# Pinning TensorE to program order in a routed-attention and feed-forward kernel, with the second product in twos and the row maxima in the ffn's PSUM banks

## The chip, the cores and the metric

The kernel runs on one core of a Trainium2 chip. A core has five engines with a queue each: TensorE (PE in the profile; its weight loads are shown as PEld), VectorE (DVE), ScalarE (ACT), GpSimd (POOL) and SyncE (SP), which here only issues DMAs. The metric is the device time of one execution in microseconds (us), lower is better.

## The reference

Routing attention over B=4 batches, H=8 heads, S=768 positions, D=64, then a feed-forward block over the 3072 tokens with 512 features:

```python
q_assign = argmax(normalised q . normalised centroids)      # 16 clusters
k_assign = argmax(normalised k . normalised centroids)
mask = q_assign[:, :, :, None] == k_assign[:, :, None, :]
scores = where(mask, scale * q @ k.T, -1e9)
attn = exp(scores - scores.max(-1)); attn /= attn.sum(-1) + 1e-9
x = (attn @ v)  as (B*S, H*D)
h = x @ w_in                                   # 512 -> 2048
out = (h * erf(softplus(h))) @ w_out           # 2048 -> 512
```

## The kernel before

Heads are worked two at a time: a *pair* p of 16, four to a batch. A pair has 12 *units* u (two halves of 384 query columns, six key tiles j each), and the main loop takes two units per iteration, 96 iterations in all. In the kernel's text, and so in the order in which it emits instructions, one iteration is:

- `scores(u)`, `scores(u + 1)`: four matmuls each into a two-bank PSUM tile `sc` of pool `ps_s` (two buffers). Two are float32 (q times k), two bf16, which add the cluster mask and a shift. ACT then writes the exponential into `pr`, one of eight buffers, and POOL adds it into `acc`.
- `attend` of the six units before, when j is 0: twelve `av` products, the sums `psum` (from `acc`), the reciprocal `den` and the writing of `xT`, the attention output that is the ffn's input. `av` has one PSUM buffer; `psum` shares a single one (tag `t`) with all transposes.
- five *slots*. Each calls `pump`, which takes ffn matmuls from the generator `stream` to about 3340 cycles' worth (`owed` carries what is over or under); `prepare`, which advances the conversion of the weights (32 steps, on ACT, DVE and POOL); and one step of `aside(p + 1)`.

`aside(p + 1)` readies the next pair in 22 steps. `route` does four steps of transposing q and k (`pt`, with three ACT copies each), `psim` against the centroids, the transposes of `sims`, a chain over DVE and POOL to the one-hot masks `aq` and `ak`, and their transposes `pb` into `qm` and `km`. `shift` does twelve steps, each two bf16 products `sm` and one DVE maximum `nmx`; then `nm`, its transpose `pn`, and a DMA to DRAM (`line`) and two back into `qm`. The next pair's second score product needs that row.

The ffn works in 12 chunks of 256 tokens, three to a batch. `hidden(n)` is 64 products `hp` with w_in, then `gate(n)` on ACT and DVE; `project(n)` is 32 products `po` with w_out. Both take PSUM from `ps_f`, two banks. The stream yields nothing until all four pairs of the batch are done; from the 17th product of a chunk on, it mixes in two products of the chunk before's `project` for each `hp`. `xT` has few buffers: chunk c of pair p takes the slot of pair p - 5 (p - 6 for the third chunk), and waits until that one's `hidden` has read it.

The framework's scheduler sets the final order in each engine's queue when the program is built. The order of emission is a priority; an instruction that the scheduler takes to be ready may go ahead of earlier ones that it takes to be waiting. This holds for all engines.

The lines that the prediction names: L242 `pt`, L251 and L253 their copies, L260 `psim`, L270 the transposes of `sims`, L275 to L287 the chain on DVE (POOL in between), L301 `pb`, L311 the copy to `km`, L323 `sm`, L327 `nmx`, L332 `nm`, L337 `pn`, L364 and L370 the scores, L375 the exponential, L379 and L383 `acc`, L394 `av`, L401 `psum`, L405 and L406 `den`, L415 `xT`, L433 and L435 the gate, L454 `hp`, L475 `po`, and L155 the last step of a weight conversion.

Of the kernel before, what the change touches and what calls it, by code (L numbers as in the profile page):

```python
# [8 lines left out]
F32 = mybir.dt.float32  # L9
# [8 lines left out]
P = 128  # L18
# [25 lines left out]
def kernel(  # L44
# [8 lines left out]
    out: bass.AP,  # L53
):
    nc = tc.nc

    def pool(name, bufs, **kw):
        return ctx.enter_context(tc.tile_pool(name=name, bufs=bufs, **kw))
# [159 lines left out]
    for e in range(2):  # L218
        nc.vector.tensor_scalar_mul(out=cn[:, e], in0=cen, scalar1=rden)
    pct = ps_t.tile([P, P], F32, name="pct", tag="t")  # L220
    nc.tensor.transpose(out=pct, in_=cn.rearrange("p e d -> p (e d)"), identity=ident)
    for e in range(2):
        nc.vector.tensor_copy(
            out=ccT[e * D : (e + 1) * D, :, e * C : (e + 1) * C],
# [8 lines left out]
    def route(p):  # L233
        st = pairs[p]
        for nm in "qk":
            raw = rowp.tile([P, S], F32, name=nm + "T")

            low = rowp.tile([P, 2, S], BF16, name=nm + "m")
            for half in range(2):
                pt = ps_t.tile([P, HJ, P], F32, name="pt", tag="t")  # L240
                for jj in range(HJ):
                    nc.tensor.transpose(  # L242
                        out=pt[:, jj], in_=st[nm][:, HJ * half + jj].rearrange("p e d -> p (e d)"),
                        identity=ident,
                    )
                cols = slice(half * HW, (half + 1) * HW)
                src = pt.rearrange("p j t -> p (j t)")
                own = [(slice(e * D, (e + 1) * D), low[(1 - e) * D : (2 - e) * D, e, cols]) for e in range(2)]
                for r, dst in [(slice(0, P), raw[:, cols])] + own:
                    if nm == "q":  # L250
                        nc.scalar.mul(out=dst, in_=src[r], mul=D**-0.5)  # L251
                    else:
                        nc.scalar.copy(out=dst, in_=src[r])  # L253
                yield
            st[nm + "T"], st[nm + "m"] = raw, low
            del st[nm]
        load_qk(p + 1)
        psim = ps_t.tile([P, HW], F32, name="psim", tag="t")
        for g in range(4):
            nc.tensor.matmul(  # L260
                psim[2 * C * g : 2 * C * (g + 1)], lhsT=ccT[:, p % HP],
                rhs=st["qk"[g // 2] + "T"][:, (g % 2) * HW : (g % 2 + 1) * HW],
                start=True, stop=True,
            )
        sims = routep.tile([P, HW], F32, name="sims")
        nc.scalar.copy(out=sims, in_=psim)
        yield
        pt = ps_t.tile([P, HJ, P], F32, name="pt", tag="t")
        for jj in range(HJ):
            nc.tensor.transpose(out=pt[:, jj], in_=sims[:, jj * P : (jj + 1) * P], identity=ident)  # L270

        n = HJ * 8
        sim = pt.rearrange("p j (g c) -> p (j g) c", c=C)
        mx = routep.tile([P, n], F32, name="mx")
        nc.vector.reduce_max(out=mx, in_=sim, axis=AX.X)  # L275
        oh = sims.rearrange("p (g c) -> p g c", c=C)
        nc.vector.tensor_tensor(
            out=oh, in0=sim, in1=mx.unsqueeze(2).to_broadcast([P, n, C]), op=ALU.is_equal
        )

        nc.gpsimd.tensor_tensor(
            out=oh, in0=oh, in1=rank.unsqueeze(1).to_broadcast([P, n, C]), op=ALU.mult
        )
        mr = routep.tile([P, n], F32, name="mr")
        nc.vector.reduce_max(out=mr, in_=oh, axis=AX.X)
        for i, (dst, op) in enumerate(((aq, ALU.is_equal), (ak, ALU.not_equal))):
            nc.vector.tensor_tensor(  # L287
                out=dst.rearrange("p j h e c -> p j (h e) c")[:, :, :, 0:C],
                in0=oh.rearrange("p (j x g) c -> p j x g c", j=HJ, x=2)[:, :, i],
                in1=mr.rearrange("p (j x g) -> p j x g", j=HJ, x=2)[:, :, i].unsqueeze(3).to_broadcast(  # L290
                    [P, HJ, 4, C]
                ),
                op=op,
            )
        yield
        yield

        for nm, src in (("qm", aq), ("km", ak)):
            pb = ps_t.tile([P, NJ, P], BF16, name="pb", tag="t")
            for j in range(NJ):  # L300
                nc.tensor.transpose(  # L301
                    out=pb[:, j], in_=src[:, j % HJ, j // HJ].rearrange("p e c -> p (e c)"),
                    identity=identb,
                )
            for e in range(2):
                r = slice(e * D, (e + 1) * D)
                src = pb[r].rearrange("p j t -> p (j t)")
                if nm == "qm":
                    nc.vector.tensor_scalar_mul(out=st[nm][r, e], in0=src, scalar1=-BIG)
                else:  # L310
                    nc.scalar.copy(out=st[nm][r, e], in_=src)  # L311
            yield
# [3 lines left out]
    def shift(p):  # L316
        st = pairs[p]
        nmx = small.tile([P, NJ, 2, 2], F32, name="nmx")
        for t in range(NJ):
            for half in range(2):  # L320
                sm = ps_s.tile([P, 2, 512], F32, name="sm", tag="s")
                for e in range(2):
                    nc.tensor.matmul(  # L323
                        sm[:, e, 0:HW], lhsT=st["qm"][:, e, t * P : (t + 1) * P],
                        rhs=st["km"][:, e, half * HW : (half + 1) * HW], start=True, stop=True,
                    )
                nc.vector.tensor_reduce(  # L327
                    out=nmx[:, t, half], in_=sm[:, :, 0:HW], axis=AX.X, op=ALU.max, negate=True
                )
                yield  # L330
        nm = small.tile([P, 2, NJ], BF16, name="nm")
        nc.vector.scalar_tensor_tensor(  # L332
            out=nm.rearrange("p e t -> p t e"), in0=nmx[:, :, 0], scalar=FLOOR, in1=nmx[:, :, 1],
            op0=ALU.min, op1=ALU.min,
        )
        pn = ps_t.tile([2 * NJ, P], BF16, name="pn", tag="t")
        nc.tensor.transpose(out=pn, in_=nm.rearrange("p e t -> p (e t)"), identity=identb)  # L337
        nmT = small.tile([2 * NJ, P], BF16, name="nmT")
        nc.scalar.copy(out=nmT, in_=pn)
        line = linep.tile([2 * NJ, P], BF16, name="line")  # L340
        nc.sync.dma_start(out=line, in_=nmT)
        for e in range(2):
            r = e * D + SH
            nc.sync.dma_start(
                out=st["qm"][r : r + 1, e],
                in_=line[e * NJ : (e + 1) * NJ].rearrange("(o t) p -> o (t p)", o=1),
            )
        load(p, "v", v, vp)
        yield
# [7 lines left out]
    def scores(u):  # L357
# [3 lines left out]
        cols = slice(half * HW, (half + 1) * HW)  # L361
        for e in range(2):
            r = slice(e * D, (e + 1) * D)
            nc.tensor.matmul(  # L364
                sc[:, e, 0:HW], lhsT=st["kT"][r, j * P : (j + 1) * P], rhs=st["qT"][r, cols],
                start=True, stop=False,
            )
        for e in range(2):
            r = slice(e * D, (e + 1) * D)
            nc.tensor.matmul(  # L370
                sc[:, e, 0:HW], lhsT=st["km"][r, e, j * P : (j + 1) * P], rhs=st["qm"][r, e, cols],
                start=False, stop=True,
            )
# [10 lines left out]
                out=st["acc", half], in0=st["acc", half], in1=pr[:, :, 0:HW], op=ALU.add  # L384
            )

    def attend(u0):

        p, half, _ = units[u0]
        st = pairs[p]  # L390
        av = ps_v.tile([P, HW + 2], F32, name="av")
        for j in range(NJ):
            for e in range(2):
                nc.tensor.matmul(  # L394
                    av[e * D : (e + 1) * D], lhsT=st["v"][:, j, e], rhs=prs[(u0 + j) % NPT][:, e],
                    start=(j == 0), stop=(j == NJ - 1),
                )

        psum = ps_t.tile([P, HW], F32, name="psum", tag="t")
        for e in range(2):  # L400
            nc.tensor.matmul(  # L401
                psum[e * D : (e + 1) * D], lhsT=ones, rhs=st["acc", half][:, e], start=True, stop=True
            )
        den = routep.tile([P, HW], F32, name="den")
# [4 lines left out]
        while lo < (half + 1) * HW:  # L409
            c = lo // TB  # L410
            hi = min((c + 1) * TB, (half + 1) * HW)
            if c not in x:
                x[c] = xTp.tile([P, TB], F32, name=f"xT{c}", bufs=XBUFS[c])
            own = slice(lo - half * HW, hi - half * HW)
            nc.vector.scalar_tensor_tensor(  # L415
# [4 lines left out]
        if half == 1:  # L420
            xTs[p] = pairs.pop(p)["x"]


    TJ = TB // P
    CPB = S // TB

# [17 lines left out]
    def hidden(n):  # L444
        b, c = n // CPB, n % CPB
        gs[n] = gp.tile([P, NFT, TB], F32, name="g")
        for fp in range(NFT // GW):
# [3 lines left out]
            for a in range(GW):  # L451
                f0 = (fp * GW + a) * P
                for r in range(HP):
                    nc.tensor.matmul(  # L454
                        hp[:, a], lhsT=w_in[:, r, f0 : f0 + P],
                        rhs=xTs[b * HP + r][c],
                        start=(r == 0), stop=(r == HP - 1),
# [3 lines left out]
            nc.vector.tensor_copy(out=gs[n][:, fp * GW : (fp + 1) * GW], in_=hp)  # L461
            if fp == NFT // GW - 1:
                gate(n)
            yield 4 * TB

    out_v = out.rearrange("(b p j) m -> b j p m", p=P, j=NJ)

    def project(n):
        b, c = n // CPB, n % CPB
        for tt in range(TJ):  # L470
            po = ps_f.tile([P, DM], F32, name="po", tag="f")
            for ft in range(NFT):
                while converted[0] < DM // P * (DFF // LC) + ft + 1:
                    yield None
                nc.tensor.matmul(  # L475
                    po, lhsT=gs[n][:, ft, tt * P : (tt + 1) * P], rhs=w_out[:, ft],
                    start=(ft == 0), stop=(ft == NFT - 1),
                )
# [64 lines left out]
    for u in range(0, nu, 2):  # L543
# [2 lines left out]
            ahead = aside(p + 1)  # L546
        scores(u)
        scores(u + 1)
        if j == 0 and u:
            attend(u - NJ)  # L550
        for _ in range(SLOTS):
            if len(xTs) >= HP:
# [38 lines left out]
```

## Time and profile before

| | |
|---|---|
| runs | 1399.59, 1400.01, 1400.53 us; median 1400.01 |
| profiled execution | 1399.7 us, its span 1397.9 us |
| PE busy | 1253.9 us (90%), 5313 instructions |
| DVE, ACT, POOL busy | 605.1 (43%), 533.5 (38%), 337.0 (24%) us |
| mean granted PE clock | 0.961 |
| the chain that ended last | PE 68%, ACT 7%, DVE 5% of the span |
| first exp of pairs 0, 1, 2, 3, 4 | 65.3, 128.1, 199.6, 271.2, 322.1 us |

The page's shares are averages over a first stage without ffn work, a long stage in which attention and ffn share PE, and a last one with ffn only. So the profile is read by stages. A wait is written "who waited, its line <- what released it". In a timeline line, "x12" is twelve instructions merged, and a bracket gives the idle time before them. A float32 product appears as two matmul instructions.

### The profile page before, as it was taken

What the parts mean: (1) busy time and instruction counts of PE and PEld (TensorE: products, weight loads), DVE (VectorE), ACT (ScalarE), POOL (GpSimd) and SP (SyncE); (2) the same over time, 40 slices, a digit from 0 to 9 for tenths busy, and PEclk for the clock granted to TensorE, in tenths of its full rate; (3) what the DMA queues carried; (4) which work ended last, traced back from release to release, by engine and by line L of the source; (5) the groups of instructions that cost most, each with busy time, mean ns of one, the idle gap of its engine ahead of it and who ended that gap; (6) DMA issues with size and microseconds to landing.
All of it is one profiled execution on the core that took longest, in us unless ns stands there. A gap on an engine that the chain in (4) does not pass through costs nothing.

```text
span 1397.9 us, 13314 instructions
## 1 busy us (share of the span) xinstructions
PE 1253.9 (90%) x5313; PEld 659.5 (47%) x5313; DVE 605.1 (43%) x827; ACT 533.5 (38%) x672; POOL 337.0 (24%) x225
## 2 busy tenths in 40 slices
PE   2566666779999999999999999999999999999998
PEld 1222222225645545454645644554646446565764
DVE  5777777643625343525343342525342342221211
ACT  4434434325534515432533425433523524321311
POOL 2244343423222222231222132222221222100000
PEclk9987777889999999999999999999999999999999
DMA  5322222101010101010100101010100000000000
GB/s 145 101 72 81 74 72 82 36 14 34 1 42 8 35 8 31 12 35 8 31 12 16 34 8 42 1 42 8 34 8 8 12 8 8 0 15 8 8 15 15
DMA packets 83982, 42.94 MB, mean 31 GB/s; under 512 B 76720, under 2 KB 76752, under 8 KB 83920
## 3 DMA queue, kind: packets, MB, share of 16 engines
q1 hardware_dynamic: 83920, 42.08, 11.1%
q8 instruction: 42, 0.69, 0.2%
q14 instruction: 20, 0.16, 0.0%
HBM read 35.73 MB, written 6.34 MB: 30 GB/s over the span
## 4 chain that ended last, share of the span: by engine, by line
PE 68%; ACT 7%; DVE 5%; issue 2%; POOL 2%; POOLq 0%; ACTq 0%; DVEq 0%
PE po L475 23%; PE hp L454 19%; PE sc L364 8%; PE av L394 8%; PE sm L323 4%; PE sc L370 2%; PE psum L401 1%; PE pt L242 1%; DVE nmx L327 1%; POOL acc L383 1%; ACT pr L375 1%; DVE den L406 1%; ACT qm L251 1%; ACT a_s L435 1%; PE pb L301 1%
## 5 line engine op out<-in xcount | busy, mean ns | idle before, releaser
L454 PE MATMUL hp<-xT,w_in 128*128 128x256 f32 x1536 | 383.4, 386 | 12.0 <-DVE xT L415 12.0
L475 PE MATMUL po<-w_out,g 128*128 128x512 f32 x768 | 369.5, 598 | 0.0
L383 POOL TENSOR_TENSOR acc<-acc,pr 128x768 f32<-128x768 f32 x128 | 218.4, 1706 | 522.6 <-ACT pr L375 512.0
L454 PEld LDWEIGHTS hp<-xT,w_in 128*128 128x128 f32 x1536 | 283.5, 191 | 124.2 <-issue 79.2
L375 ACT ACTIVATE pr<-sc 128x768 f32<-128x768 f32 x192 | 152.4, 811 | 262.9 <-PE sc L370 261.1
L327 DVE TENSOR_REDUCE nmx<-sm 128x2 f32<-128x768 f32 x192 | 181.3, 952 | 140.8 <-PE sm L323 140.4
L364 PE MATMUL sc<-qT,kT 64*128 64x384 f32 x768 | 205.0, 560 | 9.0 <-ACT pr L375 4.1
L475 PEld LDWEIGHTS po<-w_out,g 128*128 128x128 f32 x768 | 139.4, 190 | 106.6 <-issue 94.4
L461 DVE COPY g<-hp 128x512 f32<-128x512 f32 x96 | 65.9, 686 | 254.3 <-PE hp L454 253.8
L394 PE MATMUL av<-pr,in_v 128*64 128x386 f32 x768 | 170.4, 514 | 4.9 <-DVE xT L415 4.9
L406 DVE RECIPROCAL den<-den 128x384 f32<-128x384 f32 x32 | 81.6, 2549 | 133.6 <-ACT den L405 133.6
L323 PE MATMUL sm<-km,qm 128*128 128x384 bf16 x384 | 104.5, 352 | 16.7 <-DVE nmx L327 11.4
L364 PEld LDWEIGHTS sc<-qT,kT 64*128 64x128 f32 x768 | 74.4, 199 | 94.3 <-issue 50.4
L433 ACT ACTIVATE a_s<-g 128x2048 f32<-128x2048 f32 x24 | 45.9, 1911 | 184.7 <-DVE g L461 184.6
L379 POOL TENSOR_TENSOR acc<-pr,pr 128x768 f32<-128x768 f32 x32 | 58.2, 1819 | 176.7 <-ACT pr L375 170.3
L394 PEld LDWEIGHTS av<-pr,in_v 128*64 128x64 f32 x768 | 55.2, 139 | 88.1 <-issue 80.4
L323 PEld LDWEIGHTS <-qm 128*128 128x128 bf16 x384 | 34.1, 101 | 106.0 <-issue 97.5
L437 DVE TENSOR_TENSOR g<-a_s,g 128x512 f32<-128x512 f32 x96 | 61.8, 701 | 47.7 <-ACT a_s L435 47.4
L370 PE MATMUL sc<-qm,km 64*128 64x384 bf16 x384 | 76.8, 342 | 0.0
L189 POOL TENSOR_TENSOR a_s<-a_s 128x512 f32<-128x512 f32 x32 | 41.6, 1302 | 105.2 <-DVE a_s L186 86.9
L405 ACT ACTIVATE den<-psum,alleps 128x384 f32<-128x384 f32 x32 | 18.6, 581 | 113.5 <-PE psum L401 81.0
L311 ACT COPY km<-pb 64x768 bf16<-64x768 bf16 x32 | 25.4, 793 | 92.2 <-PE pb L301 91.8
(77 smaller groups left out, 769.3 us busy)
## 6 DMA issues: line engine op xcount, KB each, us to landing
a_s<-in_moe_w_in_dram SPq DMA_DIRECT2D x16, 512.0 KB
a_s<-in_moe_w_out_dram SPq DMA_DIRECT2D x16, 512.0 KB
in_q<-in_q_dram SPq DMA_DIRECT2D x32, 192.0 KB
in_k<-in_k_dram SPq DMA_DIRECT2D x32, 192.0 KB
in_v<-in_v_dram SPq DMA_DIRECT2D x32, 192.0 KB
out_dram<-osb SPq DMA_DIRECT2D x24, 256.0 KB
qm<-line SPq DMA_DIRECT2D x32, 1.5 KB
line<-nmT SPq DMA_DIRECT2D x16, 3.0 KB
```

Source lines behind the costliest of these rows:

```text
L323: nc.tensor.matmul(sm[:, e, 0:HW], lhsT=st["qm"][:, e, t * P : (t + 1) * P], rhs=st["km"][:, e, half * HW : (half + 1) * HW], start=True, ...
L327: nc.vector.tensor_reduce(out=nmx[:, t, half], in_=sm[:, :, 0:HW], axis=AX.X, op=ALU.max, negate=True)
L364: nc.tensor.matmul(sc[:, e, 0:HW], lhsT=st["kT"][r, j * P : (j + 1) * P], rhs=st["qT"][r, cols], start=True, stop=False,)
L370: nc.tensor.matmul(sc[:, e, 0:HW], lhsT=st["km"][r, e, j * P : (j + 1) * P], rhs=st["qm"][r, e, cols], start=False, stop=True,)
L375: nc.scalar.activation(out=pr[:, :, 0:HW], in_=sc[:, :, 0:HW], func=ACT.Exp)
L383: nc.gpsimd.tensor_tensor(out=st["acc", half], in0=st["acc", half], in1=pr[:, :, 0:HW], op=ALU.add)
L394: nc.tensor.matmul(av[e * D : (e + 1) * D], lhsT=st["v"][:, j, e], rhs=prs[(u0 + j) % NPT][:, e], start=(j == 0), stop=(j == NJ - 1),)
L406: nc.vector.reciprocal(out=den, in_=den)
L437: nc.vector.tensor_tensor(out=h[:, i : i + GW], in0=s[i // half][:, i % half : i % half + GW], in1=h[:, i : i + GW], op=ALU.mult,)
L454: nc.tensor.matmul(hp[:, a], lhsT=w_in[:, r, f0 : f0 + P], rhs=xTs[b * HP + r][c], start=(r == 0), stop=(r == HP - 1),)
L461: nc.vector.tensor_copy(out=gs[n][:, fp * GW : (fp + 1) * GW], in_=hp)
L475: nc.tensor.matmul(po, lhsT=gs[n][:, ft, tt * P : (tt + 1) * P], rhs=w_out[:, ft], start=(ft == 0), stop=(ft == NFT - 1),)
```

## The change

- Every matmul and transpose now goes through a helper that pins it behind the PE instruction emitted before it. PE's queue is then exactly in emission order. The other engines are scheduled as before.
- In the first four pairs (up to u=48) `attend` no longer comes as one bunch of six units: each iteration emits the `av` products of the two units before, behind its own two scores, and the third time also the sums and `xT`. Later pairs keep the bunch.
- For pairs 1 to 4, whose `shift` runs before the ffn has begun, the two products `sm` go to two one-bank tiles `sm1` in `ps_f`, with one 384-wide maximum each, where it was one two-bank tile in `ps_s` and one maximum over both.
- Before a slot of `xT` is taken, `catch_up` advances the ffn stream until the `hidden` that reads the slot's last content has been emitted. With PE in program order, that `hidden` could not run otherwise.

```diff
+    def matmul(*args, **kw):
+        tc.keep_in_program_order(nc.tensor.matmul(*args, **kw))
+
+    def transpose(**kw):
+        tc.keep_in_program_order(nc.tensor.transpose(**kw))
...
             for half in range(2):
-                sm = ps_s.tile([P, 2, 512], F32, name="sm", tag="s")
+                cols = slice(half * HW, (half + 1) * HW)
+                if p == 0 or p > HP:
+                    both = ps_s.tile([P, 2, 512], F32, name="sm", tag="s")
+                    sm = [both[:, e, 0:HW] for e in range(2)]
+                else:
+                    sm = [ps_f.tile([P, HW], F32, name="sm1", tag="f") for e in range(2)]
                 for e in range(2):
-                    nc.tensor.matmul(
-                        sm[:, e, 0:HW], lhsT=st["qm"][:, e, t * P : (t + 1) * P],
-                        rhs=st["km"][:, e, half * HW : (half + 1) * HW], start=True, stop=True,
+                    matmul(
+                        sm[e], lhsT=st["qm"][:, e, t * P : (t + 1) * P], rhs=st["km"][:, e, cols],
+                        start=True, stop=True,
                     )
-                nc.vector.tensor_reduce(
-                    out=nmx[:, t, half], in_=sm[:, :, 0:HW], axis=AX.X, op=ALU.max, negate=True
-                )
+                if p == 0 or p > HP:
+                    nc.vector.tensor_reduce(
+                        out=nmx[:, t, half], in_=both[:, :, 0:HW], axis=AX.X, op=ALU.max, negate=True
+                    )
+                else:
+                    for e in range(2):
+                        nc.vector.tensor_reduce(
+                            out=nmx[:, t, half, e : e + 1], in_=sm[e], axis=AX.X, op=ALU.max,
+                            negate=True,
+                        )
...
-    def attend(u0):
+    def attend(u0, js=range(NJ)):
...
+        if js[0] == 0:
+            st["av"] = ps_v.tile([P, HW + 2], F32, name="av")
+        av = st["av"]
+        for j in js:
...
+        if js[-1] < NJ - 1:
+            return
...
             if c not in x:
+                catch_up(p - XBUFS[c], c)
                 x[c] = xTp.tile([P, TB], F32, name=f"xT{c}", bufs=XBUFS[c])
...
+    def catch_up(p, c):
+
+        while p >= 0 and hidden_done[0] <= p // HP * CPB + c:
+            if next(stream) is None:
+                next(conv)
...
             if fp == NFT // GW - 1:
                 gate(n)
+                hidden_done[0] = n + 1
...
-        if j == 0 and u:
+        if 0 < u <= HP * 2 * NJ:
+            attend((u - 2) // NJ * NJ, range((u - 2) % NJ, (u - 2) % NJ + 2))
+        elif u and j == 0:
             attend(u - NJ)
```

## The prediction

> **What bounds the kernel now.** First the page's slices, for where TensorE (PE) is short of work:
>
> ```profile
> PE   2566666779999999999999999999999999999998
> PEclk9987777889999999999999999999999999999999
> ```
>
> Slices are 35 us. Up to slice 9 PE is 50 to 70% busy and its granted clock is reduced; then it is full. Cut by stage (columns: us; busy time, with instruction counts, of PE, weight load, DVE, ACT, POOL; granted clock; DMA share; GB/s):
>
> ```profile
> 128.00:199.60 71.60, 48.09 (x194) 17.89 (x192) 53.41 (x66) 28.99 (x46) 29.75 (x20) 0.76 0.25 76
> 271.20:322.10 50.90, 41.02 (x189) 16.08 (x190) 22.32 (x27) 18.76 (x30) 17.08 (x12) 0.87 0.10 24
> 322.10:1204.00 881.90, 855.95 (x3873) 464.02 (x3872) 347.40 (x453) 368.14 (x446) 218.02 (x132) 1.00 0.08 19
> 546.90:602.90 56.00, 51.63 (x266) 26.19 (x264) 27.80 (x37) 26.26 (x37) 16.58 (x11) 1.00 0.10 22
> 1204.00:1398.00 194.00, 190.21 (x616) 117.50 (x616) 39.44 (x58) 38.79 (x25) 0.00 (x0) 0.99 0.03 11
> ```
>
> Pair 1 (first exp at 128.0 to the next pair's at 199.6) has no ffn beside it and takes 71.6 us, no engine full: it is a chain of waits. Pair 3, where the weight conversions are nearly over, takes 50.9. From 322 to 1204 PE idles for 25.9 us in 881.9: there PE's work is the time. After 1204 only ffn is left, in program order already, and PE idles 3.8 us. So what a change adds to PE's idle time after 322 is paid in full.
>
> Who held PE up, in the first stage and then in the full one (us in total, times, longest):
>
> ```profile
> PE pn L337 <- DVE nm L332: 18.2, 3, 6.1
> PE pb L301 <- DVE aq L287: 17.3, 4, 5.7
> ```
>
> ```profile
> PE pt L242 <- ACT qm L251: 5.6, 13, 1.3
> PE pb L301 <- DVE aq L287: 3.1, 5, 0.9
> ```
>
> The routing step costs PE 4.3 us a pair at `pb` in the first stage and 3.1 us in all later. The chain is the same; later something else fills it. The timeline shows what (start, us, engine):
>
> ```profile
> 564.64 0.49 PE L270 MATMUL pt<-ident,sims 128*128 128x128 f32 x3
> 564.97 2.75 PE L454 MATMUL hp<-xT,w_in 128*128 128x256 f32 x12
> 567.66 0.86 PE L394 MATMUL av<-pr,in_v 128*64 128x386 f32 x2
> 568.57 0.51 PE L301 MATMUL pb<-identb,aq 128*128 128x128 bf16 x6
> 569.00 1.52 PE L394 MATMUL av<-pr,in_v 128*64 128x386 f32 x8
> 570.49 0.51 PE L301 MATMUL pb<-identb,ak 128*128 128x128 bf16 x6
> 570.92 1.51 PE L394 MATMUL av<-pr,in_v 128*64 128x386 f32 x6
> 572.37 1.99 PE L454 MATMUL hp<-xT,w_in 128*128 128x256 f32 x8
> ```
>
> Those `av` products are emitted three iterations later (after the scores of u=90), and the `hp` at 572.37 belongs to batch 1, emitted after u=96, whose exp is at 602.9. The scheduler pulled both forward into holes. The pin forbids exactly this. Prices of the filler come from the tail:
>
> ```profile
> 1352.76 13.98 PE L454 MATMUL hp<-xT,w_in 128*128 128x256 f32 x64
> 1366.58 27.63 PE L475 MATMUL po<-w_out,g 128*128 128x512 f32 x64
> ```
>
> Two instructions make one product (float32): 0.432 us for `hp` (13.82 us from start to start, over 32) and 0.863 for `po`.
>
> **Part 1, the emission order, by counting the loop.** An iteration (two units) pumps 5 x 3340 cycles, at 1024 for an `hp` and 2048 for a `po`: 16.7 kcycles, about 7 us. A chunk is 65.5 kcycles of `hidden` and 65.5 of `project`; batch 0 offers 3 + 2 of these (328 kcycles), later batches 3 + 3 (393). `catch_up` runs the stream until hidden(1), hidden(4), hidden(7) are emitted, before `xT1` of pairs 5, 9, 13 (u=66, 114, 162). hidden(1) needs 64 + 64 `hp` and 32 `po`, 197 kcycles; nine iterations gave about 150, so 39 products (34 `hp`, 5 `po`) come in one bunch. At u=114 and 162 it is 42 `hp` and 20 `po`. The bunch isn't taken off `owed`, so pumping goes on at the old rate, and the 131 kcycles left are gone after 7.9 iterations: the stream is dry at u=82 to 94, 130 to 142, 178 to 190, seven iterations in each batch, where before's order was dry for about four and a half, two and a half and two and a half. In a dry stretch a pinned PE has attention alone.
>
> **Part 2, a dry pair** (7, and 11; pair 15 has no routing of a next pair). The nearest row is pair 3 of before, 50.9 us in free order. Pinned, walked by its rows: `pt` of q began 4.4 us after the pair's scores; now scores 2.5, `av` and `psum` 1.9, `den` 0.7, so +1. The second scores and `av` (2.5 + 0.9) stand between `psim` and the transposes of `sims`, 0.5 to 1 of it beside the ACT copy: +2.4. From the first `sm` (292.3) to `pn` (317.8) it took 25.5; in order it is 12 steps of 1.23, scores three times 2.5, products and sums about 5 and `den` with `xT` 3.3, less 3 of overlap: 27.5, +2. With rounding and a lower clock 58 us. PE needs 32 for such a pair: 856 us busy, less 470 for 576 `hp` and 256 `po`, less 14 of hidden(9), over 12 pairs, and one more as pair 15 is cheaper. So 26 idle, twice, and 2 in pair 15: **54 us**. Ends: 51 a pair (38 in all) and 68 (74).
>
> On the clock, the rows: granted 1.00 from 322 to 1204, 0.76 in pair 1, 0.87 in pair 3. Of the 58 us, pair 3's own 0.87 and some 2 us more are clock. The Trainium skill's "TensorE: Matmul & The Clock Gate" (Part 1, The HAM clock gate) says that about 3.4 us without activity halves PE's clock and that as long of sustained activity restores it. It speaks against this change: gaps that were covered at `pb` and `pn` would each cost, as an estimate by that page, 1.7 us or more of slowness beyond themselves, 3.4 for a dry pair, where the trace of pair 1 shows lower-clock stretches longer than one such window.
>
> **Part 3, the other iterations, pinned.** Seventeen a batch, 51 in all, 8.5 pairs. Between two steps of `aside` lies one pump, 1.4 us. A `pt` waits for three ACT copies: 2.1 to 2.7 us apart in pair 3 against 0.55 + 1.4 of cover, 0.3 each, five times 1.5. `pb` comes 4.0 us after `sims`' transposes (284.59 to 288.57) against 0.5 + 2.8, and the POOL multiply may queue behind two 1.7 us adds: 1.7. `sm` holds two buffers against a 2.55 us reciprocal and 0.75 of `xT`: 0.9, twice. That is 5.0 a pair, 42. A gate holds ACT for four passes of 1.91 us and table loads of 1.28, and `exp` and `km` copies wait; in the gate at 563 to 578 the two `km` copies lie 4.0 us apart, and PE still waited 1.47 with free order. I take 2 us for each of nine gates: 18. Sum **60**. Ends: 26, as idle as now, and 110 (6.5 a pair, 6 a gate). The 25.9 idle now is in neither and goes off.
>
> **Part 4, the first stage.** Pinning: +5 a pair as in part 2, +20. `sm1` in `ps_f` leaves `ps_s` to the scores: 1.3 us a pair (twelve steps at 1.12 for two 0.56 us reduces, the rate of the 128x384 `mx` reduce at L275, against 1.23), -5; scores no longer wait for `nmx` (6.3 us in the profile), -5. Products in twos: the same matmuls, nothing added; they shorten the bunch before `psum`, counted above. 96 short reduces replace 48 of 0.95: +8 us of DVE, beside DVE's 30% idle time; uncovered it is 2 a pair. `aside`'s DMAs (`line`, two to `qm`, `v`) stay in the same steps; behind a later `pn` waits the next pair's second score product, and it is in the walk. The 18.2 us at `pn` come from weight conversions ordered ahead of `nm` on DVE; they may go or grow. I take **+10**, ends -30 and +35.
>
> **The sum.** The profiled execution is 1399.7 (span 1397.9 and 1.8 around it), the median of three 1400.01, so 0.3 apart. 1399.7 + 10 + 54 + 60 - 26 = **1497.7**, say 1498. The lowest ends of all give 1408, the highest 1593.
>
> **Rivals.**
> - Faster: the first stage gives more than the dry stretches take. If pairs 0 to 2 (63.0, 71.6, 71.6) all came down to pair 3's 50.9, that is -53.5; with dry pairs at 51 (+38) and filled iterations 6 better than now: 1378. It decides when ffn can start before about 290 instead of 322. For it: DVE and PE idle there, scores and maxima share two buffers. Against: the waits at `pb` and `nm` are chains that the change leaves as they are. 0.10.
> - Only the dry stretches count, and filled iterations are as full as now, because one pump covers each step: about 1445. For it: 1.4 us against stalls of 0.3. Against: the trace shows PE using work from far ahead. 0.25.
> - Gates and lower clock: dry pairs at 68, six a gate: 1575. 0.12.
> - No effect, because the order before is nearly the program's (hidden(2) ended at 568, as emission has it): 1400. Against: batch 1's `hp` thirty us early. 0.03.
>
> The forecast has 0.50. **Range** 1420 to 1575: it leaves out the faster rival, no effect and the outer parts of the others, some 0.2. Faster by over 0.2% (2.8 us, about what a measurement tells from no change) 0.10, within 0.03, slower 0.87.
>
> **What would show it.** Granted clock below 1 and PE near 60% in the stretches of pairs 7 and 11, less in 15; two ffn bunches of some 35 us with no scores; PE waits at `pb` and `pt` of tens of us after 322. The sum is wrong in part 2 if pairs 7 and 11 stay near 45 us, in part 3 if PE's idle time outside the dry stretches is under 30, in part 4 if pair 4's first exp comes before 300. A PE as full as now from 322 on would refute the forecast.

## The result, and the profile after

The changed kernel takes 1543.79 us (median of 4, 1543.45 to 1545.58) against 1399.8; the ratio is 1.1032, interval 1.1013 to 1.1051. The profiled execution's span is 1542.3 us, 144.4 more than before. The page's slices, now of 38.6 us:

```profile
PE   3364456668999997589989997589979998899999
PEclk9977677879999998789999999689999999999999
```

PE is as busy as before in total (1256.1 us against 1253.9), so 142 of the 144 us are time in which it idles (286.2 against 144.0). The first stage is longer and emptier, and two dents stand at slices 16 to 18 and 25 to 27 (counted from 1), with the granted clock down in both. By stage (us; busy PE, weight load, DVE, ACT, POOL; clock; DMA share; GB/s), in the order pair 1, pair 3, first exp of pair 4 to the last exp, pair 7, the rest:

```profile
146.00:235.00 89.00, 46.28 (x190) 17.82 (x188) 65.96 (x92) 31.75 (x50) 35.34 (x23) 0.69 0.23 73
295.80:357.40 61.60, 41.61 (x190) 16.43 (x188) 22.41 (x38) 18.96 (x30) 18.04 (x12) 0.75 0.09 20
357.40:1336.70 979.30, 862.36 (x3842) 475.46 (x3840) 346.63 (x452) 363.72 (x441) 212.56 (x130) 0.94 0.07 17
606.40:673.10 66.70, 43.29 (x190) 18.57 (x192) 22.34 (x27) 19.00 (x32) 18.65 (x12) 0.70 0.08 18
1336.70:1542.30 205.60, 198.99 (x666) 122.43 (x662) 40.14 (x59) 38.93 (x26) 4.11 (x3) 1.00 0.03 11
```

The whole first stage and the shared stretch of before, then the first stage of the change:

```profile
65.30:322.10 256.80, 182.02 (x745) 67.71 (x747) 172.87 (x215) 98.69 (x155) 104.13 (x67) 0.79 0.21 60
322.10:1199.90 877.80, 853.77 (x3863) 463.31 (x3862) 347.40 (x453) 368.02 (x445) 215.08 (x131) 1.00 0.08 19
```

```profile
62.90:357.40 294.50, 173.47 (x739) 67.19 (x738) 177.95 (x263) 103.31 (x164) 105.06 (x67) 0.75 0.19 54
```

Pair 1 went from 71.6 to 89.0 us and pair 3 from 50.9 to 61.6, but pair 2 from 71.6 to 60.8: the change issues its last weight transfer at 226.5 us, in pair 1, where before issued it at 259.1, in pair 2, so its pairs 0 and 1 hold more of the conversions. In the shared stretch PE idles 116.9 us, where before (first exp of pair 4, 322.1, to the last exp's end, 1199.9) it idled 24.0. Pair 7 is now attention alone. Added up: the start to pair 0's first exp -2.4, first stage 256.9 to 294.5, +37.6, shared stretch 877.7 to 979.3, +101.6, tail 198.1 to 205.6, +7.5; together 144.3.

What PE waits for in the shared stretch (us in total, times, longest):

```profile
PE sc L59 <- ACT pr L394: 20.8, 9, 4.3
PE pt L62 <- ACT qm L258: 20.6, 12, 6.1
PE pb L62 <- DVE aq L294: 19.1, 8, 5.2
PE sm L59 <- DVE nmx L340: 11.6, 13, 2.8
PE pn L62 <- DVE nm L351: 9.6, 7, 2.3
```

`pt` waited 5.6 us there before, `pb` 3.1. (All matmuls have L59 now and all transposes L62: the helpers' lines.) The timeline of pair 7's routing shows the hole that used to hold other work:

```profile
629.13 0.55 PE L62 MATMUL pt<-ident,sims 128*128 128x128 f32 x3
...
632.42 0.99 POOL L288 TENSOR_TENSOR sims<-sims,rank 128x384 f32<-128x384 f32 x1
...
634.45 0.82 PE L62 MATMUL pb<-identb,aq 128*128 128x128 bf16 x6 [4.76 <-DVE aq L294]
...
636.50 0.82 PE L62 MATMUL pb<-identb,ak 128*128 128x128 bf16 x6 [1.24 <-DVE qm L316]
...
638.21 0.48 PE L59 MATMUL sm<-km,qm 128*128 128x384 bf16 x1 [0.88 <-ACT km L318]
```

Before, `hp` and `av` lay in this gap; now PE is empty for 4.76 us, then waits 1.24 and 0.88. POOL's multiply stands behind two additions to `acc` (629.03 to 632.42).

### The profile page after: what moved, and what is told of

Its sections match the earlier page's. It is cut to its first block, busy times and chain, and to the rows that moved or that the text cites. A ratio compares the mean times of both kernels' runs of the same rounds, so it can differ in the third digit from the quotient of the medians.

```text
span 1542.3 us, 13384 instructions
## 1 busy us (share of the span) xinstructions
PE 1256.1 (81%) x5313; PEld 673.8 (44%) x5313; DVE 609.6 (40%) x875; ACT 530.0 (34%) x668; POOL 336.6 (22%) x225
## 4 chain that ended last, share of the span: by engine, by line
PE 63%; DVE 14%; ACT 10%; issue 4%; POOL 4%; DMA 2%; POOLq 0%; ACTq 0%; SPq 0%; DVEq 0%
PE po L59 20%; PE hp L59 17%; PE sc L59 10%; PE av L59 7%; PE sm L59 3%; DVE nmx L340 3%; POOL acc L402 2%; PE pt L62 2%; DVE den L429 2%; ACT pr L394 2%; DVE nmx L345 2%; ACT km L318 1%; ACT qm L258 1%; DMA a_s<-in_moe_w_out_dram 1%; PE psum L59 1%
## 5 line engine op out<-in xcount | busy, mean ns | idle before, releaser
L59 PE MATMUL hp<-xT,w_in 128*128 128x256 f32 x1536 | 384.0, 386 | 0.0
L59 PE MATMUL po<-w_out,g 128*128 128x512 f32 x768 | 372.5, 599 | 6.2 <-DVE osb L514 4.0
L59 PEld LDWEIGHTS hp<-xT,w_in 128*128 128x128 f32 x1536 | 287.3, 192 | 114.6 <-issue 82.3
L59 PE MATMUL sc<-qT,kT 64*128 64x384 f32 x768 | 205.2, 617 | 29.3 <-ACT pr L394 20.8
L340 DVE TENSOR_REDUCE nmx<-sm 128x2 f32<-128x768 f32 x144 | 135.7, 951 | 135.4 <-PE sm L59 134.6
L59 PEld LDWEIGHTS po<-w_out,g 128*128 128x128 f32 x768 | 140.3, 191 | 105.1 <-issue 81.8
L59 PE MATMUL sm<-km,qm 128*128 128x384 bf16 x384 | 115.6, 367 | 68.2 <-DVE nmx L345 31.7
L59 PE MATMUL av<-pr,in_v 128*64 128x386 f32 x768 | 143.3, 517 | 0.3 <-DVE xT L439 0.3
L59 PEld LDWEIGHTS sc<-qT,kT 64*128 64x128 f32 x768 | 75.2, 224 | 124.0 <-issue 61.6
L59 PEld LDWEIGHTS <-qm 128*128 128x128 bf16 x384 | 37.6, 102 | 141.4 <-issue 131.1
L59 PEld LDWEIGHTS av<-pr,in_v 128*64 128x64 f32 x768 | 53.6, 145 | 86.7 <-issue 85.9
L468 DVE TENSOR_TENSOR g<-a_s,g 128x512 f32<-128x512 f32 x96 | 61.1, 686 | 63.5 <-ACT a_s L466 63.2
L59 PE MATMUL sc<-qm,km 64*128 64x384 bf16 x384 | 73.1, 371 | 4.3 <-DMA qm<-line 4.3
L345 DVE TENSOR_REDUCE nmx<-sm 128x1 f32<-128x384 f32 x96 | 48.9, 549 | 32.6 <-PE sm L59 30.4
```

The source lines that it names most:

```text
L59: tc.keep_in_program_order(nc.tensor.matmul(*args, **kw))
L340: nc.vector.tensor_reduce(out=nmx[:, t, half], in_=both[:, :, 0:HW], axis=AX.X, op=ALU.max, negate=True)
L345: nc.vector.tensor_reduce(out=nmx[:, t, half, e : e + 1], in_=sm[e], axis=AX.X, op=ALU.max, negate=True,)
L468: nc.vector.tensor_tensor(out=h[:, i : i + GW], in0=s[i // half][:, i % half : i % half + GW], in1=h[:, i : i + GW], op=ALU.mult,)
```

## The experiments

Twelve runs; each ratio is to runs of before made beside it. "First stage" is from pair 0's first exp to pair 4's, "shared" from there to the end of the last exp. All times beside a total are from the profiled execution.

| run | total, median | ratio to before (95%) | first stage | shared | PE idle, first / shared |
|---|---|---|---|---|---|
| before | 1399.8 | | 256.9 | 877.7 | 75 / 24 |
| the change | 1543.8 | 1.1032 (1.1013 to 1.1051) | 294.5 | 979.3 | 121 / 117 |
| pin_alone | 1533.1 | 1.0950 (1.0934 to 1.0966) | 284.9 | 977.7 | 121 / 116 |
| pin_sm1 | 1541.9 | 1.1016 (1.0982 to 1.1050) | 288.5 | 981.5 | 120 / 117 |
| pin_first | 1463.2 | 1.0450 (1.0433 to 1.0468) | 295.4 | 905.8 | 122 / 45 |
| pin_later | 1488.5 | 1.0631 (1.0610 to 1.0653) | 233.8 | 978.3 | 46 / 117 |
| no_pin | 1401.9 | 1.0026 (1.0013 to 1.0039) | 234.5 | 899.7 | 41 / 45 |
| paced | 1481.8 | 1.0583 (1.0569 to 1.0598) | 294.2 | 916.6 | 121 / 72 |
| conv_order | 1537.5 | 1.0982 (1.0967 to 1.0998) | 276.7 | 990.3 | 101 / 126 |
| noconv_pin | 1485.4 | 1.0612 (1.0575 to 1.0649) | 247.5 | 980.1 | 83 / 117 |
| noconv_free | 1337.7 | 0.9557 (0.9517 to 0.9596) | 209.7 | 875.9 | 23 / 24 |
| free_parts | 1371.5 | 0.9791 (0.9769 to 0.9812) | 233.6 | 873.3 | 42 / 24 |
| free_sm1 | 1371.5 | 0.9803 (0.9785 to 0.9821) | 233.6 | 874.4 | 46 / 24 |
| free_sm1_conv | 1373.7 | 0.9818 (0.9789 to 0.9846) | 226.2 | 884.8 | 37 / 32 |

**no_pin.** All of the change, without the pin (the transposes likewise):

```diff
     def matmul(*args, **kw):
-        tc.keep_in_program_order(nc.tensor.matmul(*args, **kw))
+        nc.tensor.matmul(*args, **kw)
```

> All of the change but the pin: the products in twos, the maxima in ps_f and catch_up stay, TensorE is in free order. Theory (the pin carries the loss, 117 us of idle time from the first exp of pair 4 to the end of attention against 24 before): the scheduler fills the dry stretches and the holes again, 1385 to 1415 us, PE idle in that part under 35. Rival (the bunches that catch_up emits leave the stream dry whatever the order of PE): 1420 to 1460, with PE idle 60 or more.

Measured 1401.9: the theory's total. But it is made of two things that the theory had not: the first stage is 22.4 us shorter than before, and the shared one 22 longer, with 45 us of idle time, which lies between the two forecasts.

```profile
65.50:300.00 234.50, 193.11 (x767) 68.32 (x767) 173.69 (x267) 102.16 (x162) 103.78 (x67) 0.87 0.23 68
300.00:1199.70 899.70, 854.82 (x3813) 463.88 (x3814) 346.37 (x448) 359.02 (x434) 211.66 (x129) 0.98 0.07 18
```

So two parts of the change cancel when the pin is away, and adding the pin to them costs 142 us.

**pin_first and pin_later.** The pin for one stage only:

```diff
+        ins = nc.tensor.matmul(*args, **kw)
+        if at[0] < 48:          # pin_later: >= 48
+            tc.keep_in_program_order(ins)
```

> The pin holds only for what is emitted before u=48, so in the first stage; later instructions are in free order, the rest as in the change. Theory: the first stage stays at its 294 us from the first exp of pair 0 to that of pair 4 (257 before), the later part returns to before's: 1425 to 1445 us. Rival (the first stage's loss comes from the products in twos or the split maxima, not from the pin): the same here, but then the run without any pin is as slow in its first stage as this one.

> The pin holds only from u=48 on; the first stage is in free order. Theory: first stage near before's 257 us or somewhat under, the later part keeps the 101 us that it lost, and the tail 7: 1490 to 1515 us. Rival (a pinned later part is slow because of what the first stage leaves behind, conversions and late transfers): under 1460.

pin_first's two stages, then pin_later's:

```profile
62.90:358.20 295.30, 173.62 (x742) 67.73 (x742) 176.19 (x263) 103.40 (x164) 105.30 (x67) 0.75 0.18 54
358.20:1264.00 905.80, 861.29 (x3850) 467.73 (x3848) 350.24 (x452) 362.74 (x441) 212.86 (x130) 0.99 0.07 19
```

```profile
65.50:299.30 233.80, 187.68 (x727) 64.16 (x729) 172.56 (x263) 98.30 (x155) 103.79 (x67) 0.85 0.22 66
299.30:1277.60 978.30, 860.90 (x3842) 475.42 (x3841) 345.79 (x452) 363.55 (x441) 211.41 (x129) 0.94 0.07 17
```

The first stage is 295 us pinned and 234 free, the shared stretch 978 pinned and 906 free. So the stages' losses stand by themselves and add up. pin_first's total was missed upward (1463 against 1425 to 1445), because its free shared stretch didn't return to before's 878; pin_later's was just missed downward (1488.5), because the free first stage is 23 us better than before's.

**pin_alone and pin_sm1.** The first-stage parts undone, then only the twos:

```diff
-                if p == 0 or p > HP:
+                if True:                     # pin_alone: both places
...
-        if 0 < u <= HP * 2 * NJ:
+        if False:                            # both runs
```

> The pin and catch_up alone: attend comes as one bunch of six units in every pair, and the maxima go through the two-bank tile in ps_s in every pair. Theory: these two parts are worth little, since the chains at pb, pt and pn hold the first stage: 1530 to 1565 us. Rival (they mend what the pin does to the first stage, where scores and maxima in one pool would wait for each other in strict order): 1580 to 1620, all of it before the first exp of pair 4.

> The change without the products in twos: pin, catch_up and the maxima in ps_f. It lies between the change (1543.8) and the pin alone (1533.1). Theory (the two reduces of 0.55 us for one of 0.95 sit in a DVE queue full of conversions, and in strict order PE stands behind them): it keeps the 10 us, 1540 to 1548. Rival (the twos put av in front of the routing steps and cost it): 1530 to 1536.

Under the pin the two parts make the kernel slower, by 10.7 us together (1533.1 against 1543.8). By the totals the maxima carry 8.9 of it; the twos have 1.9, inside the runs' spread. Pairs 2 and 3, without conversions, gain 2 to 3 us each from both parts (63.5 and 63.5 in pin_alone, 60.8 and 61.6), pairs 0 and 1 lose 7 each (76.1 and 81.8 against 83.1 and 89.0).

The theory for pin_sm1 met the total (1541.9), but its cause, the extra maxima among the conversions, is not borne out by the pairs. With the maxima alone in ps_f, pairs 0 and 1 take 77.3 and 84.6, 1.2 and 2.8 more than in pin_alone; the twos then add 5.8 and 4.4, as the rival had it for these pairs, and the gain of pairs 2 and 3 comes with them as well (63.4 and 63.2 in pin_sm1). The first stage is 284.9, 288.5 and 294.5 us, and 3.8 of what the maxima cost lies in the shared stretch, where the two kernels are written alike. These are single profiled executions a few us apart, and why either part costs anything under the pin stays open. Pair 1 of pin_alone, then of pin_sm1:

```profile
139.20:221.00 81.80, 42.05 (x180) 18.25 (x178) 61.75 (x81) 33.13 (x54) 33.66 (x23) 0.67 0.27 85
```

```profile
141.00:225.60 84.60, 46.38 (x192) 18.82 (x190) 63.94 (x94) 33.12 (x54) 33.80 (x22) 0.68 0.26 82
```

**free_parts and free_sm1.** From no_pin, `catch_up` taken out; then the twos as well:

```diff
             if c not in x:
-                catch_up(p - XBUFS[c], c)
...
-        if 0 < u <= HP * 2 * NJ:             # free_sm1 only
+        if False:
```

> No pin and no catch_up: before with only the products in twos and the maxima in ps_f for the first four pairs. Theory (without the pin these two take 22 us off the first stage, 256.9 to 234.5, and the run without the pin lost as much later only through catch_up's bunches, 899.7 against 877.7): 1374 to 1382 us, PE idle after the first exp of pair 4 back to 24. Rival (the later part lengthens because it starts earlier with the same transfers and xT buffers): 1392 to 1402.

> The run before (no pin, no catch_up) without the products in twos: only the maxima go to ps_f. Theory (the maxima sharing ps_s with the scores is what held the first stage): most of the 22 us stays, first stage 234 to 242. Rival (the twos do it, by freeing pr buffers and PE's bunch earlier): first stage 250 or more, total within 6 us of before.

Both beat the kernel before, by 28 us, and are equal to each other: the maxima in `ps_f` are the whole gain, and the twos give nothing. Whether it is the other PSUM pool or the split into two maxima, no run separates. Taking `catch_up` out brought the shared stretch from 899.7 to 873.3 and its idle time from 45 to 24, so the bunches cost 26 us even in free order. The shared stretch of free_parts:

```profile
300.00:1173.30 873.30, 848.85 (x3839) 461.43 (x3840) 343.75 (x449) 364.55 (x438) 213.48 (x130) 1.00 0.08 19
```

free_sm1's pair 1, whole first stage and shared stretch:

```profile
126.90:185.30 58.40, 47.52 (x189) 16.88 (x188) 47.59 (x71) 26.70 (x44) 26.20 (x17) 0.82 0.27 75
65.70:299.30 233.60, 187.75 (x760) 68.90 (x760) 181.63 (x266) 100.83 (x159) 103.13 (x67) 0.85 0.24 67
299.30:1173.70 874.40, 850.74 (x3846) 462.83 (x3847) 344.38 (x450) 365.98 (x441) 213.59 (x130) 1.00 0.08 19
```

And PE's longest waits in that first stage:

```profile
PE pb L62 <- DVE aq L294: 17.1, 4, 6.1
PE pt L62 <- ACT qm L258: 9.5, 6, 1.6
PE sc L59 <- ACT pr L394: 6.1, 6, 1.8
PE sm L59 <- DVE nmx L345: 6.0, 8, 2.1
```

The 18.2 us at `pn` are gone from the list; the 17.1 at `pb` stand as before. Two more waits of before's first stage are gone, 15.5 us together:

```profile
PE hp L454 <- DVE xT L415: 10.6, 4, 3.0
PE av L394 <- DVE xT L415: 4.9, 3, 2.3
```

In their place PE waits 6.1 us at `sc` and 6.0 at `sm`. So what comes behind the maxima no longer holds PE, and the routing chain still does.

**paced.** Pinned, the stream spread over the whole batch, with other `xT` slots so that the bunches nearly go (two small ones stay, 15 and 9 products):

```diff
-XBUFS = (5, 5, 6)
+XBUFS = (5, 6, 7)                            # outp: 1 buffer
...
-                pump(per_slot)
+                pump(first if u < 96 else per_slot)   # 2731, then 3277 cycles
...
-        owed[0] = min(owed[0], 8 * cycles)
+        owed[0] = min(owed[0], 2 * cycles)
```

> The change with the pin, but the ffn spread evenly over a batch: xT slots 5, 6, 7 where they were 5, 5, 6 (one osb buffer to make room), 2731 cycles per slot in the first batch and 3277 in the later ones. By the emission order the stream is then dry in one iteration of a batch where it was in seven. Theory (of the 117 us of PE idle time in the later part some 70 lie in the dry stretches, pairs 7 and 11 alone 47): idle time falls by 45 to 55, total 1488 to 1500. Rival (strict order costs as much in every iteration, whether ffn stands between or not): 1520 or more.

```profile
357.30:1273.90 916.60, 844.27 (x3858) 463.47 (x3854) 344.91 (x452) 366.67 (x443) 215.84 (x131) 0.98 0.07 19
```

Idle time in the shared stretch fell from 117 to 72 us and the stretch by 62.7; PE's busy time fell by 18 as the clock rose from 0.94 to 0.98. The fall in idle time, 44.6, is just under the 45 to 55 forecast, and the total, 1481.8, is 6 under the theory's range. So the dry stretches, with the bunches ahead of them, cost 62 us; the run takes both away together. 72 idle us remain in strict order with work spread evenly: 1.0 per iteration.

**conv_order.** The change, with ACT's two passes of a weight conversion in ACT's program order (the second pass likewise):

```diff
-            nc.scalar.activation(out=xf, in_=hi.bitcast(F32), func=ACT.Square)
+            tc.keep_in_program_order(nc.scalar.activation(out=xf, in_=hi.bitcast(F32), func=ACT.Square))
```

> The change, with the two ACT passes of each weight conversion pinned in ACT's order too, so that they don't stand ahead of routing's copies. In the change ACT waits 51 us for weight transfers in pairs 0 and 1 and PE stands behind it (pt 6.6 us behind den, 4.9 behind a copy). Theory (that is over half of what the pin costs in the first stage, as the pinned pairs with conversions take 83 and 89 us and those without 61): first stage 294.5 to 250 to 270, total 1518 to 1528. Rival (the chain in strict order alone makes it): within 6 us of the change.

It starts from this wait of the change in pairs 0 and 1, which was 14.9 us in before's:

```profile
ACT a_s L174 <- DMA a_s<-in_moe_w_out_dram: 42.7, 13, 8.6
...
ACT a_s L174 <- DMA a_s<-in_moe_w_in_dram: 8.3, 2, 6.4
```

With the edit 2.1 us of it are left, and pairs 0 and 1 take 68.1 and 69.4 us. But the conversions now run on into pairs 2 and 3 (70.5 and 68.8 against 60.8 and 61.6) and pair 4 (86.0 against 75.3). Of 17.8 us, 11 came back later; the total moved by 6. The waits for transfers were real but mostly moved work, and the theory was wrong on its size.

**noconv_pin and noconv_free.** The conversion replaced by one copy, pinned and free:

```diff
-            nc.scalar.activation(out=xf, in_=hi.bitcast(F32), func=ACT.Square)
...
+            nc.vector.tensor_copy(out=w_steps[n][0].bitcast(U32), in_=raw[:, :, 1])
```

> The change with the weight conversion left out: each step loads its block and one DVE copy of its high words takes the place of two ACT, five DVE and one POOL instruction (the weights are cut, not rounded). Read together with the same kernel in free order. Theory (of the 60 us that the pin costs in the first stage most comes from what the conversions do to the other engines' queues, since the two pinned pairs without conversions take 61 us each and the two with them 83 and 89): first stage pinned 235 to 250, free 205 to 230, 10 to 30 apart. Rival (strict order by itself): 45 to 60 apart.

> The run with both first-stage parts, no pin and no catch_up, with the weight conversion left out in the same way. Theory: first stage 205 to 230 us, that is 10 to 30 under the pinned one. Rival: 45 to 60 under it.

The two first stages, pinned and then free:

```profile
50.60:298.10 247.50, 164.16 (x742) 64.44 (x742) 96.13 (x167) 75.23 (x120) 70.98 (x44) 0.79 0.18 54
```

```profile
54.60:264.30 209.70, 186.68 (x749) 64.70 (x750) 103.51 (x168) 69.44 (x108) 72.16 (x44) 0.89 0.22 66
```

247.5 and 209.7: 37.8 apart, between the two forecasts. So of the 61 us that the pin costs in the first stage (233.6 to 294.5), 38 are strict order by itself, 9.4 a pair, and 23 come only with the conversions beside it. PE's longest waits in them, in the same order:

```profile
PE sm L59 <- DVE nmx L322: 22.3, 36, 2.5
PE pb L62 <- DVE aq L271: 16.6, 4, 5.3
PE pt L62 <- ACT qm L235: 12.6, 8, 1.6
PE pt L62 <- ACT km L237: 6.2, 4, 1.5
PE psim L59 <- ACT km L237: 6.1, 4, 1.5
```

```profile
PE pb L62 <- DVE aq L271: 12.0, 4, 3.4
PE pt L62 <- ACT qm L235: 6.6, 5, 1.6
PE pt L62 <- ACT den L405: 2.0, 3, 0.7
```

In strict order PE stands 36 times at `sm` for a maximum, and at the ACT copies (12.6, 6.2 and 6.1 us); in free order other work fills most of this, and the long chain at `pb` is the main wait left.

**free_sm1_conv.** free_sm1 with conv_order's edit:

> Free order, only the maxima moved to ps_f, and the ACT passes of the conversions in ACT's program order. Theory (ACT's 11 us of waits for weight transfers in pairs 0 to 2 go, nothing else moves): first stage 224 to 230, total 1360 to 1368. Rival (the conversions end later and are given back from pair 3 on, as in the pinned run with this edit): 1369 to 1380.

The first stage came out as the theory had it, 226.2, and the shared stretch gave it back, pair 4 above all (76.6 us with 10.0 idle, against 68.1 with 1.7). The total, 1373.7, lies in the rival's range: no gain. The waits for weight transfers in free_sm1's pairs 0 to 2, 11 us in the expectation, are 29.0 in its trace. The best kernels found are free_sm1 and free_parts, 2% under before.

## Why the prediction was right, point by point

The time lies in the range and the sign is right; the size was 98 forecast and 144 measured, a third short. Of the 46 us that were missing, 27.6 lie in the first stage, 13.6 in the shared stretch (88 forecast, 101.6 measured) and 7.5 in the tail; the start gave 2.4 back. Term by term:

- **Dry stretches, part 2.** Forecast 54 us of idle time. Over the iterations that part 1 counts as dry (u=82 to 94, 130 to 142, 178 to 190) the trace has 60.9: pairs 7 and 11 idle 23.4 and 23.3 (26 forecast), pair 15 0.9 (2 forecast), and 13.3 lie in the iterations u=82, 130 and 178, just before these pairs, which the walk left out. In paced, where only u=142 and 190 are dry, 22.4 are left in the same iterations. The pairs took 66.7 and 66.5 us where the walk had 58. That their idle time came near is partly luck: pair 7 is 8.7 us longer than the walk, but PE is also busy for 43.3 us of it, where the sum took 32.
- **Filled iterations, part 3.** Forecast 60; measured 116.9 - 60.9 = 56.0. Over the whole stretch, dry pairs included, the named waits are the ones found (`pt` 20.6, `pb` 19.1, `sc` for the exponential 20.8).
- **The sum of both** was near, 114 forecast and 116.9 measured, with 7 too few in one term and 4 too many in the other. But idle time isn't all: PE's busy time in the stretch rose by 8.6 us (853.8 to 862.4) with the clock at 0.94, and the tail by 7.5, since free order had begun 12 of the last batch's `hp` products ahead of the last exp (384 instructions of `hp` now stand in the tail, 360 before). The sum had neither.
- **First stage, part 4: the term that failed.** Forecast +10 as +20 for the pin and -10 for the maxima. Measured +37.6, and the two terms don't add. Without the pin the parts give -23, and the pin on top of them +61. Taken the other way round, the first stage of pin_alone is 28 over before's, and the parts add 10 under the pin. So the pin's +20 was 8 short by itself, the gain of the maxima was more than twice as large in free order, and that it would turn into a loss under the pin was in no term (2 us a pair for the longer maxima, if uncovered, is named and not counted); there the sum failed. The walk gave 5 us a pair for what scores and `av` add when they stand in the chain and not in its holes; the pinned and free runs without conversions differ by 9.4. The conversions' share, 23, was not in the sum. The gain of the maxima was taken from 6.3 us of waits on `nmx` and the DVE cadence. Those 6.3 us are idle time of the weight loads (PEld); no product of PE's scores waits for `nmx` in that stage. What went with the maxima in free order was the 18.2 us at `pn`, which the prediction left at nought, and 15.5 at `hp` and `av`, which it didn't list.
- **`catch_up`.** Its effect was counted right in the emission order, but as a thing that matters only under the pin. no_pin against free_parts shows 26 us in free order too.
- **The clock.** The Trainium skill's "TensorE: Matmul & The Clock Gate" (Part 1, The HAM clock gate) says that about 3.4 us without activity takes the clock to half. The trace agrees in kind: pair 7's mean granted clock is 0.70, with gaps at PE of 4.8 us (`pb`) and 3.5 (`sc`), where the covered pair 7 of before had 1.00. In this pair the trace's clock records are full or half only, half for 39 of the 66.7 us. The estimate from that page, 3.4 us a dry pair, is under the 8.7 by which the pair exceeded the walk; how much of the 8.7 is clock no run separates.
- **Rivals.** "Faster" was wrong under the pin, but its mechanism is real: with no pin the first stage does end at 299 to 300, and without `catch_up` as well the kernel is 28 us faster. "Only the dry stretches count" is refuted by the 56 us of the filled iterations (17 in before's) and by paced. "Gates and lower clock" had the length of the dry pairs, 68, and the low clock there, but at 1575 too much in all. Two of the rivals' times don't follow from the prediction's own terms, which give 1464 where it has 1445, and 1554 where it has 1575.
- **Two readings of before's trace.** The `av` products in pair 7's routing are emitted two iterations later, not three. From 322 to 1204 there are 1159 instructions of `hp`, that is 579.5 products; beyond the 576 counted they are worth 1.5 us and not 14, which moves the 32 by one. Nothing else rests on either.

## What to carry to other kernels

Here, pinning PE to the order of emission turned waits of short chains into idle time of PE: 75 to 121 us in the first stage (pin_alone), 24 to 117 in the shared one. Price such a change by what the trace shows in the holes now, and by counting where the emission order runs out of filler. Undo a change part by part in both settings: here the one useful part (the maxima in idle PSUM banks, -28 us) cost 9 us under the pin, and was hidden by two losses, the pin's and that of `catch_up`.

## What was not expected of the hardware

ACT stood still for 51 us for weight transfers in pairs 0 and 1 of the change, up to 8.6 us at a time, against 14.9 in pairs 0 and 1 before; both kernels load the same 32 blocks of 512 KB, before some of them later. ACT ran nothing else in those 51 us, yet they were a poor measure of the cost. Removing them gained only 6 us in all, because the same conversions then fell elsewhere. And in free order free_sm1, with 29.0 us of such waits in pairs 0 to 2, is as fast as free_parts with 16.7.
